# Token-halved first tiles, reordered loads, paired gate products and norm steps on another engine, in a fused state-space and gated-MLP kernel

## The chip, the cores and the metric

One core of one Trainium2 chip. The metric is the device time of one execution in microseconds (us), as the median of several executions. A profile of one execution goes with each kernel; its span (first to last instruction) is 1.8 to 1.9 us shorter than the time measured for that execution. Engines: PE is TensorE's matmuls, PEld its weight loads, DVE is VectorE, ACT is ScalarE, POOL is GpSimd, SP is SyncE, which issues the DMAs (SPq is its queue).

## The reference, cut to what matters

```python
# x: (1, 2048, 512); w_gate, w_up: (512, 1376); w_down: (1376, 512); all bfloat16
xn = layernorm(x)
# state-space layer: diagonal complex recurrence over 2048 tokens
Bu = xn @ (((Lam_bar - 1) / Lam)[:, None] * B).T
for t in range(L):
    h = Lam_bar * h + Bu[t]
s = 2 * (hseq @ C.T).real + xn * Dskip
g = silu((gelu(xn @ w_gate) * (xn @ w_up)) @ w_down)
return x + s * g
```

## The kernel before: the parts that matter

The 2048 tokens are four slabs of 512 (`TS`). In the loop over slabs, TensorE does, for slab s, 11 gate and up tiles of 128 features (`ffn`), and between them, after tiles 5, 7, 9 and 10, the four output matmul groups of slab s-1 (`y_mm`). Then come the scan input of slab s+1 (`u_ps`) and the down projection of slab s. ScalarE applies gelu and copies from PSUM, VectorE multiplies the two, scans, rotates and forms the outputs.

The head, slab 0: every tile of x is normalised, transposed on TensorE and copied to `xnT` before the first gate matmul:

```python
xs = [norm0(0), norm0(1)]
tps = [t_xn0(0, xs[0]), t_xn0(1, xs[1])]
xnT_out(nc.vector, 0, tps[0]); xnT_out(nc.scalar, 1, tps[1])
xs += [norm0(2), norm0(3)]
...                                   # tiles 2 and 3 the same way, then the first ffn
```

Slabs 2 and 3: ScalarE takes two sums per tile, and small steps (`ln_small`) make the scale and bias of the norm. For slab 1 VectorE takes the statistics. In all three ScalarE writes `xn`, and a DMA transposes it.

```python
def ln_out(s, m):
    ACT(out=xn[:], in_=x_tok[...], func=AF.Identity, scale=rs[...], bias=nb[...])
    nc.sync.dma_start_transpose(out=xnT[:, :, c0 : c0 + P], in_=xn[:])

def epi(s, m, y_ps, g2):
    def f():
        TT(out=yg[:], in0=y_ps[:, :], in1=g2[:], op=ALU.mult)
        TT(out=ot[:], in0=yg[:], in1=x_tok[:, s * M + m, :], op=ALU.add)
    dve(now() + 0.3, 0.95, f)
    nc.sync.dma_start(out=out_td[mg : mg + P, :], in_=ot[:])

# in the slab loop, after tile j
if 5 <= j < 5 + M:
    ln_out(s + 1, j - 5)
if j in (5, 7, 9, 10):
    epi(s - 1, m, y_mm(...), ...)
```

So the program order of SyncE's queue is, per slab: transpose 0, store 0, transposes 1 and 2, store 1, transpose 3, and so on.

VectorE's order is made when the kernel is built, by a small model of the two engines' clocks. Before an instruction asked for at `ready`, the helper places as much of the waiting scan and rotation work as the modelled clock allows:

```python
def drain(t, late):
    while waiting and max(clk["dve"], waiting[0][0]) + waiting[0][1] <= t + late:
        pop()                         # places a waiting scan or rotation step

def dve(ready, cost, f, late=0.8):
    drain(ready, late)
    clk["dve"] = max(clk["dve"], ready) + cost
    f()
```

Of the kernel before, what the change touches and what calls it, by code (L numbers as in the profile page):

```python
# [11 lines left out]
ALU = mybir.AluOpType  # L12
# [7 lines left out]
def kernel(  # L20
# [73 lines left out]
    def load_gu(i):  # L94
        a, b = CUTS[i], CUTS[i + 1]
        nc.sync.dma_start(out=wg[:, :, a:b], in_=wg_r[:, :, a:b])
        nc.sync.dma_start(out=wu[:, :, a:b], in_=wu_r[:, :, a:b])
# [8 lines left out]

    load_gu(0)
    load_gu(1)
    load_x(1)
    for h in range(2):  # L110
# [80 lines left out]
    ACT(out=pf[:], in_=pt_ps[:, :], func=AF.Copy)  # L191
    for a in (0, 2):
        for m in (a, a + 1):
            bn(0, m)
        for m in (a, a + 1):
            bn_end(0, m)
        rstd(0, a, a + 2)

    def xnT_out(eng, m, tp):
# [3 lines left out]
        else:  # L203
            eng.tensor_copy(out=o, in_=tp[:, :, :])

    xs = [norm0(0), norm0(1)]
    tps = [t_xn0(0, xs[0]), t_xn0(1, xs[1])]
    xnT_out(nc.vector, 0, tps[0])
    xnT_out(nc.scalar, 1, tps[1])
    xs += [norm0(2), norm0(3)]  # L210

    def second_half():
        tps.extend([t_xn0(2, xs[2]), t_xn0(3, xs[3])])
        xnT_out(nc.vector, 2, tps[2])
        xnT_out(nc.scalar, 3, tps[3])

    second_half()
    nc.gpsimd.tensor_tensor(out=dt_[:], in0=euler[:], in1=ldt, op=ALU.pow)
    STT(out=thn[:], in0=lim, scalar=1.0 / (2.0 * math.pi), in1=dt_[:], op0=ALU.mult, op1=ALU.mult)
# [5 lines left out]
    TSC(out=kr[:], in0=ang[:], scalar1=MAGIC, scalar2=MAGIC, op0=ALU.add, op1=ALU.subtract)  # L225
    TT(out=ang[:], in0=ang[:], in1=kr[:], op=ALU.subtract)
    STT(out=kr[:], in0=ang[:], scalar=-1.0, in1=ang[:], op0=ALU.mult, op1=ALU.max)
    ACT(out=sh[:], in_=ang[:], func=AF.Sin, scale=TWO_PI)
# [22 lines left out]
    diagI = consts.tile([P, KT, P], BF16, name="diagI")  # L251

    def coefficients():
        nre, nim, den, inv, t1, t2, t3, t4 = (
            small(n) for n in ("nre", "nim", "den", "inv", "t1", "t2", "t3", "t4")
        )
        TT(out=nre[:], in0=rho[:], in1=c1[:], op=ALU.mult)
        TT(out=nim[:], in0=rho[:], in1=s1[:], op=ALU.mult)
        TSC(out=nre[:], in0=nre[:], scalar1=-1.0, scalar2=None, op0=ALU.add)
        TT(out=den[:], in0=lre, in1=lre, op=ALU.mult)  # L260
        TT(out=t1[:], in0=lim, in1=lim, op=ALU.mult)
        TT(out=t2[:], in0=nim[:], in1=lim, op=ALU.mult)
        TT(out=t3[:], in0=nim[:], in1=lre, op=ALU.mult)
        TT(out=den[:], in0=den[:], in1=t1[:], op=ALU.add)
        TT(out=t1[:], in0=nre[:], in1=lre, op=ALU.mult)
        TT(out=t4[:], in0=nre[:], in1=lim, op=ALU.mult)
        nc.vector.reciprocal(out=inv[:], in_=den[:])
        TT(out=t1[:], in0=t1[:], in1=t2[:], op=ALU.add)
        TT(out=t3[:], in0=t3[:], in1=t4[:], op=ALU.subtract)
        TT(out=cre[:], in0=t1[:], in1=inv[:], op=ALU.mult)  # L270
        TT(out=cim[:], in0=t3[:], in1=inv[:], op=ALU.mult)
        TSC(out=cre[:], in0=cre[:], scalar1=2.0, scalar2=None, op0=ALU.mult)
        TSC(out=cim[:], in0=cim[:], scalar1=2.0, scalar2=None, op0=ALU.mult)
        TSC(out=ncre[:], in0=cre[:], scalar1=-1.0, scalar2=None, op0=ALU.mult)
        for kt in range(KT):
            TSC(out=diagI[:, kt, :], in0=ident_f[:], scalar1=dsk[:, kt : kt + 1], scalar2=None, op0=ALU.mult)

# [19 lines left out]
    def now():  # L297
        return clk["pe"]
# [120 lines left out]
    def ffn(s, j, at):  # L419
        cols = slice(s * TS, (s + 1) * TS)  # L420
        fs = min(P, F - j * P)
        fsl = slice(j * P, j * P + fs)
        g_ps = psum.tile([P, TS], FP32, name="g_ps", tag="ps")
        for kt in range(KT):
            nc.tensor.matmul(  # L425
                g_ps[:fs, :], lhsT=wg[:, kt, fsl], rhs=xnT[:, kt, cols], start=(kt == 0), stop=(kt == KT - 1)
            )
        u_ps = psum.tile([P, TS], FP32, name="up_ps", tag="ps")
        for kt in range(KT):
            nc.tensor.matmul(  # L430
                u_ps[:fs, :], lhsT=wu[:, kt, fsl], rhs=xnT[:, kt, cols], start=(kt == 0), stop=(kt == KT - 1)
            )
        pe_takes(2 * KT)
        gt = work.tile([P, TS], BF16, name="gt", tag="gt", bufs=4)
        ACT(out=gt[:fs], in_=g_ps[:fs, :], func=AF.Gelu_apprx_tanh)  # L435
        ub = work.tile([P, TS], BF16, name="ub", tag="ub", bufs=4)
        ACT(out=ub[:fs], in_=u_ps[:fs, :], func=AF.Copy)  # L437
        dve(now() + 0.9, 0.34, lambda: TT(out=at[:fs, j, :], in0=gt[:fs], in1=ub[:fs], op=ALU.mult))  # L438

# [69 lines left out]
    mq = consts.tile([P, NS, M], FP32, name="mq")  # L509
    nb = consts.tile([P, NS, M], FP32, name="nb")  # L510

    def ln_act(s, m):
# [4 lines left out]
    def ln_small(s):  # L517
        G = nc.gpsimd
        mean, var = sx[:, s, 0, :], sx[:, s, 1, :]
        G.tensor_scalar(out=mean, in0=mean, scalar1=1.0 / D, scalar2=None, op0=ALU.mult)  # L520
        G.tensor_tensor(out=mq[:, s, :], in0=mean, in1=mean, op=ALU.mult)
        G.tensor_scalar(out=var, in0=var, scalar1=1.0 / D, scalar2=EPS, op0=ALU.mult, op1=ALU.add)
        G.tensor_tensor(out=var, in0=var, in1=mq[:, s, :], op=ALU.subtract)
        G.tensor_tensor(out=rs[:, s, :], in0=var, in1=mhalf[:], op=ALU.pow)
        G.tensor_tensor(out=nb[:, s, :], in0=mean, in1=rs[:, s, :], op=ALU.mult)
        G.tensor_scalar(out=nb[:, s, :], in0=nb[:, s, :], scalar1=-1.0, scalar2=None, op0=ALU.mult)  # L526

# [6 lines left out]

    clk["pe"] = 9.0
    clk["dve"] = 10.5
    hsts, ats, g2s = {0: hst0}, {0: at0}, {}
# [6 lines left out]

    dve(11.5, 2.8, ln1_stats)
    G = nc.gpsimd
# [12 lines left out]
    for s in range(NS):  # L559
        for j in range(NFT):  # L560
            ffn(s, j, ats[s])
            if s == 0:
                if j == 0:
                    ca_wide()
                if j == 1:
                    dve(now(), 2.6, coefficients)
                if 3 <= j < 3 + M:
# [24 lines left out]
        if s < NS - 1:  # L592
            hsts[s + 1] = work.tile([P, 2, NPT, TS], BF16, name="hst", tag="hst")
            ats[s + 1] = work.tile([P, NFT, TS], BF16, name="at", tag="at")
            for h in range(2):
                chain(s + 1, h, u_pair(s + 1, h), hsts[s + 1])
            for m in range(M):
                g2s[s, m] = down(s, m, ats[s])
                if s == 0:
                    fold_c(m)  # L600
    s = NS - 1
    y0 = y_mm(s, 0, hsts[s])
# [37 lines left out]
```

## Time and profile before

| | before |
|---|---|
| time, median (lowest to highest) | 188.32 (188.29 to 188.4) us |
| span of the profiled run | 186.4 us |
| busy: TensorE / VectorE / ScalarE / GpSimd | 179.5 / 155.3 / 115.3 / 16.8 us |

TensorE is the bound: what it does not fill is lost. The prediction shows the lines for that. The columns of a timeline are start, length, engine and line, operation, operands; "..." marks lines left out, here and below.

### The profile page before, as it was taken

What the parts mean: (1) busy time and instruction counts of PE and PEld (TensorE: products, weight loads), DVE (VectorE), ACT (ScalarE), POOL (GpSimd) and SP (SyncE); (2) the same over time, 40 slices, a digit from 0 to 9 for tenths busy, and PEclk for the clock granted to TensorE, in tenths of its full rate; (3) what the DMA queues carried; (4) which work ended last, traced back from release to release, by engine and by line L of the source; (5) the groups of instructions that cost most, each with busy time, mean ns of one, the idle gap of its engine ahead of it and who ended that gap; (6) DMA issues with size and microseconds to landing.
All of it is one profiled execution on the core that took longest, in us unless ns stands there. A gap on an engine that the chain in (4) does not pass through costs nothing.

```text
span 186.4 us, 2533 instructions
## 1 busy us (share of the span) xinstructions
PE 179.5 (96%) x887; PEld 84.2 (45%) x887; DVE 155.3 (83%) x266; ACT 115.3 (62%) x208; POOL 16.8 (9%) x35
## 2 busy tenths in 40 slices
PE   7699999999999899999999999999999999999992
PEld 2344444444444344544444444544444444554452
DVE  4948999999977799999999999999999999532034
ACT  3289996677799979257259949747428733451210
POOL 3653000000000230000000080000000000000000
PEclk9999999999999999999999999999999999999999
DMA  5994924896000016200000003310000000000001
GB/s 147 336 306 105 223 49 92 221 250 203 0 0 0 0 24 91 58 28 28 0 0 5 2 0 77 91 30 29 0 0 0 0 4 28 28 30 28 32 28 57
DMA packets 24444, 12.26 MB, mean 66 GB/s; under 512 B 15760, under 2 KB 24432, under 8 KB 24432
## 3 DMA queue, kind: packets, MB, share of 16 engines
q1 hardware_dynamic: 24256, 12.03, 25.2%
q8 instruction: 7, 0.11, 0.3%
q10 hardware_dynamic: 176, 0.07, 0.1%
q14 instruction: 5, 0.04, 0.1%
HBM read 6.33 MB, written 2.10 MB: 45 GB/s over the span
## 4 chain that ended last, share of the span: by engine, by line
PE 88%; ACT 5%; DVE 4%; DMA 1%; issue 1%; ACTq 0%
PE f_ps L445 20%; PE g_ps L425 18%; PE up_ps L430 18%; PE u_ps L343 15%; PE y_ps L460 14%; PE y_ps L465 2%; ACT junk L515 1%; DVE st L154 1%; DMA x_tok<-in_A_x_dram 1%; PE y_ps L493 1%; ACT gt L435 1%; ACT ub L437 1%; ACT L435 1%; DVE qq L359 1%; PE tp L174 1%
## 5 line engine op out<-in xcount | busy, mean ns | idle before, releaser
L425 PE MATMUL g_ps<-xnT,wg 128*128 128x512 bf16 (+1 forms) x176 | 45.2, 379 | 0.7 <-ACT xnT L202 0.7
L430 PE MATMUL up_ps<-xnT,wu 128*128 128x512 bf16 (+1 forms) x176 | 45.2, 379 | 0.0
L445 PE MATMUL f_ps<-wd,at 128*128 128x512 bf16 (+1 forms) x176 | 38.7, 379 | 0.0
L435 ACT ACTIVATE gt<-g_ps 128x512 bf16<-128x512 f32 (+1 forms) x44 | 26.4, 600 | 11.1 <-PE g_ps L425 8.6
L389 DVE TENSOR_TENSOR_SCAN Ft<-rho,it,Wt 128x512 bf16<-128x512 f32 x24 | 30.1, 1274 | 0.0
L437 ACT ACTIVATE ub<-up_ps 128x512 bf16<-128x512 f32 (+1 forms) x44 | 26.5, 602 | 5.1 <-PE up_ps L430 4.9
L460 PE MATMUL y_ps<-C,hst 128*128 128x512 bf16 x120 | 28.7, 379 | 0.5 <-DVE hst L363 0.5
L343 PE MATMUL u_ps<-xnT,BT 128*128 128x512 bf16 x128 | 28.4, 379 | 0.0
L430 PEld LDWEIGHTS <-wu 128*128 128x128 bf16 (+1 forms) x176 | 17.6, 100 | 20.4
L445 PEld LDWEIGHTS <-at 128*128 128x128 bf16 (+1 forms) x176 | 17.2, 98 | 20.6
L348 ACT ACTIVATE U<-u_ps 128x512 bf16<-128x512 f32 x32 | 18.9, 610 | 11.1 <-PE u_ps L343 11.1
L425 PEld LDWEIGHTS <-wg 128*128 128x128 bf16 (+1 forms) x176 | 17.1, 100 | 19.0 <-issue 0.8
L438 DVE TENSOR_TENSOR at<-gt,ub 128x512 bf16<-128x512 bf16 (+1 forms) x44 | 18.0, 414 | 7.3 <-ACT ub L437 7.0
L450 ACT ACTIVATE g<-f_ps 128x512 f32<-128x512 f32 x16 | 9.6, 597 | 23.5 <-PE f_ps L445 23.5
L478 DVE TENSOR_TENSOR yg<-y_ps,g 128x512 bf16<-128x512 f32 x15 | 10.3, 684 | 13.7 <-PE y_ps L465 9.9
L343 PEld LDWEIGHTS <-BT 128*128 128x128 bf16 x128 | 12.4, 98 | 14.6
L460 PEld LDWEIGHTS <-hst 128*128 128x128 bf16 x120 | 11.5, 98 | 14.7 <-DVE hst L363 1.5
L530 ACT ACTIVATE xn<-x_tok,nb,rs 128x512 bf16<-128x512 bf16 x12 | 10.0, 832 | 3.8 <-POOL nb L526 3.8
L363 DVE TENSOR_TENSOR hst<-pp,qq 128x1024 bf16<-128x1024 bf16 x16 | 10.6, 688 | 0.2
L363 DVE TENSOR_TENSOR Wt<-pp,qq 128x1024 bf16<-128x1024 bf16 x16 | 10.5, 688 | 0.3
L515 ACT ACTIVATE junk<-x_tok 128x512 bf16<-128x512 bf16 x16 | 10.1, 630 | 0.3
L359 DVE TENSOR_TENSOR pp<-U,cos_b 128x2048 bf16<-128x2048 bf16 x8 | 9.8, 1223 | 0.3
(106 smaller groups left out, 145.0 us busy)
## 6 DMA issues: line engine op xcount, KB each, us to landing
out_dram<-ot SPq DMA_DIRECT2D x15, 128.0 KB, 1.7
x_tok<-in_A_x_dram SPq DMA_DIRECT2D x3, 512.0 KB, 6.9
wd<-in_B_w_down_dram SPq DMA_DIRECT2D x1, 1280.0 KB
wg<-in_B_w_gate_dram SPq DMA_DIRECT2D x1, 640.0 KB, 6.2
wu<-in_B_w_up_dram SPq DMA_DIRECT2D x1, 640.0 KB
wg<-in_B_w_gate_dram SPq DMA_DIRECT2D x1, 384.0 KB, 4.5
wu<-in_B_w_up_dram SPq DMA_DIRECT2D x1, 384.0 KB
wg<-in_B_w_gate_dram SPq DMA_DIRECT2D x1, 352.0 KB
```

Of the source, the lines that this page charges most:

```text
L343: nc.tensor.matmul(u_ps[:, :], lhsT=BT[:, ri, kt, pt * P : (pt + 1) * P], rhs=xnT[:, kt, cols], start=(kt == 0), stop=(kt == KT - 1),)
L348: ACT(out=U[:, ri, q, :], in_=u_ps[:, :], func=AF.Copy)
L363: return lambda: TT(out=dst()[i], in0=box["pp"][:, i, :, :], in1=box["qq"][:, 1 - i, :, :], op=op)
L389: nc.vector.tensor_tensor_scan(out=box["F"][:, ri, q, :], data0=rho[:, pt : pt + 1].to_broadcast([P, TS]), data1=box["W"][:, ri, q, :], in ...
L425: nc.tensor.matmul(g_ps[:fs, :], lhsT=wg[:, kt, fsl], rhs=xnT[:, kt, cols], start=(kt == 0), stop=(kt == KT - 1))
L430: nc.tensor.matmul(u_ps[:fs, :], lhsT=wu[:, kt, fsl], rhs=xnT[:, kt, cols], start=(kt == 0), stop=(kt == KT - 1))
L435: ACT(out=gt[:fs], in_=g_ps[:fs, :], func=AF.Gelu_apprx_tanh)
L437: ACT(out=ub[:fs], in_=u_ps[:fs, :], func=AF.Copy)
L438: dve(now() + 0.9, 0.34, lambda: TT(out=at[:fs, j, :], in0=gt[:fs], in1=ub[:fs], op=ALU.mult))
L445: nc.tensor.matmul(f_ps[:, :], lhsT=at[:fs, k, m0 : m0 + P], rhs=wd[:fs, k, :], start=(k == 0), stop=(k == NFT - 1))
L460: nc.tensor.matmul(y_ps[:, :], lhsT=hst[:, j // NPT, j % NPT, m0 : m0 + P], rhs=C2[:, j // NPT, j % NPT, :], start=(j == 0), stop=False,)
L515: ACT(out=junk[:], in_=x_tok[:, s * M + m, :], func=f, accum_out=sx[:, s, i, m : m + 1])
```

## The change

Its intent: start TensorE earlier, and take work from VectorE. The first two gate and up tiles are done in two halves of 256 tokens, so that the first halves run while tiles 2 and 3 of x are still being normalised. The x of slab 1 is loaded ahead of the second weight piece. Two gate tiles share one VectorE product of 1024 columns. The coefficients go to GpSimd (17 of 18 small steps; the reciprocal stays), the four skip diagonals to ScalarE. In exchange VectorE takes four short norm steps for each of slabs 2 and 3, which leaves GpSimd two where it had seven.

```diff
     load_gu(0)
+    load_x(1)
     load_gu(1)
-    load_x(1)
@@ head
+    for j in range(SPLIT):                       # SPLIT = 2
+        for up in range(2):
+            early[j, up] = gu_mm(0, j, up, 0, TS // 2)
+        if j == 0:
+            tps += [t_xn0(2, xs[2]), t_xn0(3, xs[3])]
+            xnT_out(nc.scalar, 3, tps[3])
   ...                                            # xnT_out(nc.vector, 2, ...) later
@@ coefficients: 17 small steps TT/TSC on VectorE -> GT/GS on GpSimd
@@ diagI: TSC on VectorE -> ACT(..., func=AF.Copy, scale=dsk[...])
@@ ffn
-        dve(now() + 0.9, 0.34, lambda: TT(out=at[:fs, j, :], in0=gt[:fs], in1=ub[:fs], op=ALU.mult))
+        if j == NFT - 1:
+            dve(now() + 0.9, 0.34, lambda: TT(...))              # the odd last tile
+        elif i:                                                  # every second tile
+            dve(now() + 0.9, 0.61, lambda: TT(out=at[:, j - 1 : j + 1, :], in0=gt[:], in1=ub[:], op=ALU.mult))
@@ ln_small
-        G.tensor_scalar(...)                      # seven steps on GpSimd
-        ...
+        def f():                                  # four steps on VectorE
+            STT(...); TSC(...); STT(...); TSC(...)
+        dve(now() + 1.0, 0.3, f)
+        nc.gpsimd.tensor_tensor(out=rs[:, s, :], in0=var, in1=mhalf[:], op=ALU.pow)
+        nc.gpsimd.tensor_tensor(out=nb[:, s, :], in0=nm[:, s, :], in1=rs[:, s, :], op=ALU.mult)
```

More of the change, by code (lines that the diff above doesn't have):

```diff
@@ L191 @@
     ACT(out=pf[:], in_=pt_ps[:, :], func=AF.Copy)
-    for a in (0, 2):
-        for m in (a, a + 1):
-            bn(0, m)
-        for m in (a, a + 1):
-            bn_end(0, m)
-        rstd(0, a, a + 2)
     def xnT_out(eng, m, tp):
@@ L204, in xnT_out @@
             eng.tensor_copy(out=o, in_=tp[:, :, :])
+    bn(0, 0)
+    bn(0, 1)
+    bn_end(0, 0)
+    bn_end(0, 1)
+    rstd(0, 0, 2)
+    nc.gpsimd.tensor_tensor(out=dt_[:], in0=euler[:], in1=ldt, op=ALU.pow)
+    bn(0, 2)
+    bn(0, 3)
     xs = [norm0(0), norm0(1)]
+    bn_end(0, 2)
+    bn_end(0, 3)
+    rstd(0, 2, 4)
     tps = [t_xn0(0, xs[0]), t_xn0(1, xs[1])]
@@ L210, with gu_mm @@
     xs += [norm0(2), norm0(3)]
-    def second_half():
-        tps.extend([t_xn0(2, xs[2]), t_xn0(3, xs[3])])
-        xnT_out(nc.vector, 2, tps[2])
-        xnT_out(nc.scalar, 3, tps[3])
-    second_half()
-    nc.gpsimd.tensor_tensor(out=dt_[:], in0=euler[:], in1=ldt, op=ALU.pow)
+    SPLIT = 2
+    early = {}
+    pair = {}
+    def gu_mm(s, j, up, a=0, b=TS, ps=None):
+        fs = min(P, F - j * P)
+        fsl = slice(j * P, j * P + fs)
+        if ps is None:
+            ps = psum.tile([P, TS], FP32, name="up_ps" if up else "g_ps", tag="ps")
+        w = wu if up else wg
+        for kt in range(KT):
+            nc.tensor.matmul(
+                ps[:fs, a:b], lhsT=w[:, kt, fsl], rhs=xnT[:, kt, s * TS + a : s * TS + b],
+                start=(kt == 0), stop=(kt == KT - 1),
+            )
+        return ps
+    for j in range(SPLIT):
[4 more added lines that the diff above has]
+            xnT_out(nc.scalar, 3, tps[3])
     STT(out=thn[:], in0=lim, scalar=1.0 / (2.0 * math.pi), in1=dt_[:], op0=ALU.mult, op1=ALU.mult)
@@ L226 @@
     TT(out=ang[:], in0=ang[:], in1=kr[:], op=ALU.subtract)
+    xnT_out(nc.vector, 2, tps[2])
     STT(out=kr[:], in0=ang[:], scalar=-1.0, in1=ang[:], op0=ALU.mult, op1=ALU.max)
@@ L251 @@
     diagI = consts.tile([P, KT, P], BF16, name="diagI")
-    def coefficients():
-        nre, nim, den, inv, t1, t2, t3, t4 = (
-            small(n) for n in ("nre", "nim", "den", "inv", "t1", "t2", "t3", "t4")
-        )
-        TT(out=nre[:], in0=rho[:], in1=c1[:], op=ALU.mult)
-        TT(out=nim[:], in0=rho[:], in1=s1[:], op=ALU.mult)
-        TSC(out=nre[:], in0=nre[:], scalar1=-1.0, scalar2=None, op0=ALU.add)
-        TT(out=den[:], in0=lre, in1=lre, op=ALU.mult)
-        TT(out=t1[:], in0=lim, in1=lim, op=ALU.mult)
-        TT(out=t2[:], in0=nim[:], in1=lim, op=ALU.mult)
-        TT(out=t3[:], in0=nim[:], in1=lre, op=ALU.mult)
-        TT(out=den[:], in0=den[:], in1=t1[:], op=ALU.add)
-        TT(out=t1[:], in0=nre[:], in1=lre, op=ALU.mult)
-        TT(out=t4[:], in0=nre[:], in1=lim, op=ALU.mult)
-        nc.vector.reciprocal(out=inv[:], in_=den[:])
-        TT(out=t1[:], in0=t1[:], in1=t2[:], op=ALU.add)
-        TT(out=t3[:], in0=t3[:], in1=t4[:], op=ALU.subtract)
-        TT(out=cre[:], in0=t1[:], in1=inv[:], op=ALU.mult)
-        TT(out=cim[:], in0=t3[:], in1=inv[:], op=ALU.mult)
-        TSC(out=cre[:], in0=cre[:], scalar1=2.0, scalar2=None, op0=ALU.mult)
-        TSC(out=cim[:], in0=cim[:], scalar1=2.0, scalar2=None, op0=ALU.mult)
-        TSC(out=ncre[:], in0=cre[:], scalar1=-1.0, scalar2=None, op0=ALU.mult)
-        for kt in range(KT):
-            TSC(out=diagI[:, kt, :], in0=ident_f[:], scalar1=dsk[:, kt : kt + 1], scalar2=None, op0=ALU.mult)
@@ new lines, with skip_diag @@
+    GT = nc.gpsimd.tensor_tensor
+    GS = nc.gpsimd.tensor_scalar
+    def skip_diag(kt):
+        ACT(out=diagI[:, kt, :], in_=ident_f[:], func=AF.Copy, scale=dsk[:, kt : kt + 1])
+    nre, nim, den, inv, t1, t2, t3, t4 = (
+        small(n) for n in ("nre", "nim", "den", "inv", "t1", "t2", "t3", "t4")
+    )
+    def coefficients():
+        GT(out=nre[:], in0=rho[:], in1=c1[:], op=ALU.mult)
+        GT(out=nim[:], in0=rho[:], in1=s1[:], op=ALU.mult)
+        GS(out=nre[:], in0=nre[:], scalar1=-1.0, scalar2=None, op0=ALU.add)
+        GT(out=den[:], in0=lre, in1=lre, op=ALU.mult)
+        GT(out=t1[:], in0=lim, in1=lim, op=ALU.mult)
+        GT(out=t2[:], in0=nim[:], in1=lim, op=ALU.mult)
+        GT(out=t3[:], in0=nim[:], in1=lre, op=ALU.mult)
+        GT(out=den[:], in0=den[:], in1=t1[:], op=ALU.add)
+        GT(out=t1[:], in0=nre[:], in1=lre, op=ALU.mult)
+        GT(out=t4[:], in0=nre[:], in1=lim, op=ALU.mult)
+        GT(out=t1[:], in0=t1[:], in1=t2[:], op=ALU.add)
+        GT(out=t3[:], in0=t3[:], in1=t4[:], op=ALU.subtract)
@@ L278, in fold_c, with coefficients_end @@
+    def coefficients_end():
+        nc.vector.reciprocal(out=inv[:], in_=den[:])
+        GT(out=cre[:], in0=t1[:], in1=inv[:], op=ALU.mult)
+        GT(out=cim[:], in0=t3[:], in1=inv[:], op=ALU.mult)
+        GS(out=cre[:], in0=cre[:], scalar1=2.0, scalar2=None, op0=ALU.mult)
+        GS(out=cim[:], in0=cim[:], scalar1=2.0, scalar2=None, op0=ALU.mult)
+        GS(out=ncre[:], in0=cre[:], scalar1=-1.0, scalar2=None, op0=ALU.mult)
     def fold_c(pt):
@@ L419, in ffn @@
     def ffn(s, j, at):
-        cols = slice(s * TS, (s + 1) * TS)
         fs = min(P, F - j * P)
-        fsl = slice(j * P, j * P + fs)
-        g_ps = psum.tile([P, TS], FP32, name="g_ps", tag="ps")
-        for kt in range(KT):
-            nc.tensor.matmul(
-                g_ps[:fs, :], lhsT=wg[:, kt, fsl], rhs=xnT[:, kt, cols], start=(kt == 0), stop=(kt == KT - 1)
-            )
-        u_ps = psum.tile([P, TS], FP32, name="up_ps", tag="ps")
-        for kt in range(KT):
-            nc.tensor.matmul(
-                u_ps[:fs, :], lhsT=wu[:, kt, fsl], rhs=xnT[:, kt, cols], start=(kt == 0), stop=(kt == KT - 1)
-            )
-        pe_takes(2 * KT)
-        gt = work.tile([P, TS], BF16, name="gt", tag="gt", bufs=4)
-        ACT(out=gt[:fs], in_=g_ps[:fs, :], func=AF.Gelu_apprx_tanh)
-        ub = work.tile([P, TS], BF16, name="ub", tag="ub", bufs=4)
-        ACT(out=ub[:fs], in_=u_ps[:fs, :], func=AF.Copy)
-        dve(now() + 0.9, 0.34, lambda: TT(out=at[:fs, j, :], in0=gt[:fs], in1=ub[:fs], op=ALU.mult))
+        if s == 0 and j < SPLIT:
+            g_ps, u_ps = (gu_mm(s, j, up, TS // 2, TS, early[j, up]) for up in range(2))
+        else:
+            g_ps, u_ps = gu_mm(s, j, 0), gu_mm(s, j, 1)
+        pe_takes(2 * KT)
+        i = j % 2
+        if i == 0:
+            pair["g"] = work.tile([P, 2, TS], BF16, name="gt", tag="gt", bufs=3)
+            pair["u"] = work.tile([P, 2, TS], BF16, name="ub", tag="ub", bufs=3)
+        gt, ub = pair["g"], pair["u"]
+        ACT(out=gt[:fs, i, :], in_=g_ps[:fs, :], func=AF.Gelu_apprx_tanh)
+        ACT(out=ub[:fs, i, :], in_=u_ps[:fs, :], func=AF.Copy)
+        if j == NFT - 1:
+            dve(now() + 0.9, 0.34, lambda: TT(out=at[:fs, j, :], in0=gt[:fs, 0, :], in1=ub[:fs, 0, :], op=ALU.mult))
+        elif i:
+            dve(now() + 0.9, 0.61, lambda: TT(out=at[:, j - 1 : j + 1, :], in0=gt[:], in1=ub[:], op=ALU.mult))
     def down(s, m, at):
@@ L510 @@
     nb = consts.tile([P, NS, M], FP32, name="nb")
+    nm = consts.tile([P, NS, M], FP32, name="nm")
     def ln_act(s, m):
@@ L517, in ln_small @@
     def ln_small(s):
-        G = nc.gpsimd
-        mean, var = sx[:, s, 0, :], sx[:, s, 1, :]
-        G.tensor_scalar(out=mean, in0=mean, scalar1=1.0 / D, scalar2=None, op0=ALU.mult)
-        G.tensor_tensor(out=mq[:, s, :], in0=mean, in1=mean, op=ALU.mult)
-        G.tensor_scalar(out=var, in0=var, scalar1=1.0 / D, scalar2=EPS, op0=ALU.mult, op1=ALU.add)
-        G.tensor_tensor(out=var, in0=var, in1=mq[:, s, :], op=ALU.subtract)
-        G.tensor_tensor(out=rs[:, s, :], in0=var, in1=mhalf[:], op=ALU.pow)
-        G.tensor_tensor(out=nb[:, s, :], in0=mean, in1=rs[:, s, :], op=ALU.mult)
-        G.tensor_scalar(out=nb[:, s, :], in0=nb[:, s, :], scalar1=-1.0, scalar2=None, op0=ALU.mult)
+        total, var = sx[:, s, 0, :], sx[:, s, 1, :]
+        def f():
+            STT(out=mq[:, s, :], in0=total, scalar=-1.0 / (D * D), in1=total, op0=ALU.mult, op1=ALU.mult)
+            TSC(out=nm[:, s, :], in0=total, scalar1=-1.0 / D, scalar2=None, op0=ALU.mult)
+            STT(out=var, in0=var, scalar=1.0 / D, in1=mq[:, s, :], op0=ALU.mult, op1=ALU.add)
+            TSC(out=var, in0=var, scalar1=EPS, scalar2=None, op0=ALU.add)
+        dve(now() + 1.0, 0.3, f)
+        nc.gpsimd.tensor_tensor(out=rs[:, s, :], in0=var, in1=mhalf[:], op=ALU.pow)
+        nc.gpsimd.tensor_tensor(out=nb[:, s, :], in0=nm[:, s, :], in1=rs[:, s, :], op=ALU.mult)
     def ln_out(s, m):
@@ L532, in ln_out @@
         nc.sync.dma_start_transpose(out=xnT[:, :, c0 : c0 + P], in_=xn[:])
-    clk["pe"] = 9.0
-    clk["dve"] = 10.5
+    clk["pe"] = 8.1
+    clk["dve"] = 10.3
     hsts, ats, g2s = {0: hst0}, {0: at0}, {}
@@ L543, in ln1_stats @@
             bn_end(1, m)
-    dve(11.5, 2.8, ln1_stats)
+    dve(10.3, 2.8, ln1_stats)
     G = nc.gpsimd
@@ L562 @@
             if s == 0:
-                if j == 0:
+                if j == 1:
                     ca_wide()
-                if j == 1:
-                    dve(now(), 2.6, coefficients)
+                    coefficients()
+                if j == 8:
+                    coefficients_end()
                 if 3 <= j < 3 + M:
@@ L600 @@
                     fold_c(m)
+                    skip_diag(m)
     s = NS - 1
```

## The prediction

> **What bounds the kernel now.** I read the busy slices first, then TensorE's own waits, then the chain of waits in order of time, then the timeline of the first 24 us and of 45 to 65 us. The slices of the page:
>
> ```profile
> PE   7699999999999899999999999999999999999992
> DVE  4948999999977799999999999999999999532034
> PEclk9999999999999999999999999999999999999999
> ```
>
> TensorE is full from the third slice to the last but one (a slice is 186.4 / 40 = 4.66 us), at the full clock: the end is set by when its matmul stream starts, by holes in it, and by a short tail. VectorE is full over long stretches too, which matters only if TensorE waits for it. TensorE's waits, as waiter, releaser, total, times and longest:
>
> ```profile
> PE w_ps L146 <- DVE halfpi L122: 1.2, 1, 1.2
> PE tp L174 <- DVE xn L165: 1.2, 2, 0.7
> PE g_ps L425 <- ACT xnT L202: 0.7, 1, 0.7
> PE y_ps L460 <- DVE hst L363: 0.5, 1, 0.5
> ```
>
> That is all. Three belong to the head: the first gate matmul waits until ScalarE has copied the last transposed tile of x (xnT). Only one is later: the first output matmul of slab 0 waits 0.5 us for hst. In the chain (start, length, piece):
>
> ```profile
> 7.79 0.73 PE tp L174 x8
> 9.19 1.02 PE g_ps L425 x4
> 10.21 0.86 PE up_ps L430 x4
> 11.08 0.86 PE g_ps L425 x4
> 11.94 0.86 PE up_ps L430 x4
> 12.80 0.86 PE g_ps L425 x4
> ...
> 61.05 1.15 DVE qq L359
> 62.22 0.70 DVE hst L363
> 62.97 1.04 PE y_ps L460 x4
> ```
>
> The stream starts at 9.19, and two gate and up tiles are through at 12.80; after that it is matmul upon matmul at 0.86 per four. From the timeline, the last matmul ends near 183.1, and product, add and store take the remaining 3.3 us. So at most two things can be won: the start (about 9.2) and the hole of 0.5. The measured 188.32 is 1.9 above the span; I keep that offset.
>
> **What the Trainium skill says.** "TensorE: Matmul & The Clock Gate", section "Back-to-back issue gap", gives N / 2.4 + 2.5 ns for a warm matmul: 215.8 ns for 512 columns and 109 for 256. The trace agrees: 0.86 / 4 = 0.216, and the 256-column output matmuls at the end (x8) take 0.87, 0.109 each. The same section's 131 ns for 512 columns in a real stream is not seen here. So halves cost no TensorE time.
>
> "VectorE: DVE Perf Modes", section "The TRN2 errata", says a fixed cost per instruction that one large tile pays once. The trace agrees:
>
> ```profile
> L438 DVE TENSOR_TENSOR at<-gt,ub 128x512 bf16<-128x512 bf16 x40 | 16.4, 414 | 6.0 <-ACT ub L437 5.8
> L363 DVE TENSOR_TENSOR hst<-pp,qq 128x1024 bf16<-128x1024 bf16 x16 | 10.6, 688 | 0.2
> ```
>
> 1024 columns cost 688 ns, two of 512 cost 828.
>
> "ScalarE: Activation LUTs", section "What ACT_TABLE_LOAD costs", has 1283 ns plus about 1380 of drain per switch. The trace has the 1283, but no such drain: the load starts at 11.29 and the first gelu at 12.59.
>
> "SBUF — State Buffer", section "Who interferes with whom", says that VectorE instructions with two SBUF inputs contend with GpSimd ones that read SBUF. It fits that the same power step on GpSimd takes 1037 ns in one place and 1466 on average in the slabs.
>
> **The change part by part.**
>
> *Head.* Before, VectorE does all statistics of slab 0 before the first norm (starts 6.08), and all four xnT tiles come before the first gate matmul. After, in steps from the timeline before (my estimate):
> - Statistics of tiles 2 and 3 end about 5.7, the first power is ready at 5.45: first norm 5.7 (was 6.08), second ends 6.43 (was 6.81).
> - From the end of a norm to its transposes done: 6.81 to 7.30, 0.49. So ScalarE copies tile 1 from 6.92 to 7.52, and the first half matmul starts at about 7.6.
> - Tile 0's gate and up halves: 8 x 0.109 + 0.16 for the cold start = 1.0, to 8.6.
> - The second power now stands behind the dt power on GpSimd (1.07) and behind the norms, so it ends near 7.7 (was 7.04); norms 2 and 3 end about 8.5, just before TensorE asks. Eight transposes to 9.1, tile 1's halves (0.87) to 10.0.
> - xnT 3 goes to ScalarE, 9.25 to 9.85. xnT 2 stands on VectorE behind the five angle steps (8.56 to 9.81 before, 1.25; now about 8.4 to 9.65), so it ends about 10.05.
> - Second halves start about 10.1 and take 16 x 0.109 = 1.74: two tiles are through at 11.85, against 12.80. **Gain 0.95**. The transposes are on the path once in both orders; what is won is that 1.9 us of matmuls fill the wait for tiles 2 and 3.
>
> *Loads.* Gate weights of the first cut land 4.5 after issue at 2.18, so at 6.7; the up weights behind them by about 7.8, from the 336 GB/s of that slice, and the up half needs them at 8.1. x of slab 1 (0.5 MB, landed at 12.75 before) moves ahead of the 1.28 MB of later weights: it lands at about 9.3, those at 11.2 and 12.9. They are first needed by tile 3 at about 13.6 and 14.4. Hidden, with 1.5 us to spare; VectorE can then start slab 1's statistics near 10.5 instead of 12.78.
>
> *VectorE.* Eighteen small coefficient steps and four diagonals leave it: 16.82 to 19.26, 2.4 us. Forty products become twenty: 16.4 - 20 x 0.688 = 2.6 us busy. Eight norm steps come, 8 x about 0.16 = 1.3. Net about -3.7, plus 2.3 from the earlier statistics. By adding the durations in the new order, I get slab 0's hst at about 57 (before: 64.0), while its first output matmul would ask at 61.9 - 0.95 = 61. In the new order hst also comes ahead of slab 1's first product, which now waits for ScalarE before it. **Gain 0.5, the hole.** All the rest of VectorE's relief is off the path and buys nothing.
>
> *ScalarE.* Four diagonals of 128x128: from 712 ns for 512 columns with a scale operand, less 384 x 0.833 = 320, some 390 ns each. Three fit in its idle 0.56 after each down block; the fourth delays slab 1's first gelu by about 0.3. Hidden, since TensorE has four tiles of PSUM lead there.
>
> *GpSimd.* Coefficients at 0.2 to 0.5 each, needed only at 45: hidden. Norm of the next slab: seven steps become two, after four short ones on VectorE; ScalarE waits for it (3.8 in total) off the path.
>
> Sum: 0.95 + 0.5 = 1.45; 188.32 - 1.45 = 186.87, **186.9**.
>
> **Rivals.**
> 1. *PSUM buffers become the wait.* The gelu table load ends at 12.59 in either order, since the sine steps end as before, so ScalarE empties tile 0 only at about 13.1, while tile 3 wants that bank at 13.6. Only 0.5 us spare. Likewise VectorE's order lets the output product of slab 1's last tile come near 83, with its bank asked for near 84. Either would return 0.2 to 0.8: 187.2 to 187.7. For it: thin margins. Against: before, TensorE waited for neither.
> 2. *Weights late.* If the up weights land at 9 rather than 7.8, or the displaced ones after 14, TensorE idles early and half of the head's gain goes: about 187.4. Against: no wait on a weight before, and bytes ahead of them are unchanged for the first cut.
> 3. *VectorE was the true limit, and its 4 us of relief count in full:* 184.5. Against: one hole of 0.5 in all of TensorE's stream after the head. I nearly exclude it.
> 4. *The pair product comes too late for the gate buffers* (three pairs instead of four singles): ScalarE would stall, then TensorE, time back to 188 or more. Against: the new order puts each pair's product at least a slab of pairs before its reuse.
>
> **Range and chances.** The two gains bound the result below: head at best 1.3 (no idle at 10.0 and an earlier first norm), with the hole 1.8, 186.5; a little is left for noise. Above, the head at 0.6 and one new wait of 0.3: 187.6. I take 186.3 to 187.7. Two per cent is 3.8 us, more than both gains together, and a loss of that size needs a stall that recurs in every slab. Hence 0.02 faster, 0.965 within, 0.015 slower.
>
> **What would show it.** In the changed profile: first gate half at 7.6 (not 9.2), third gate tile near 11.9 (not 12.8), with an idle below 0.3 us ahead of the second halves; slab 1's statistics without a wait for x; no wait of an output matmul for hst; last matmul near 181.6; VectorE's busy time some 3.5 lower with the end following only by 1.4. Wrong if TensorE's waits show ScalarE's gelu or a copy of tile 0 ahead of tile 3, a weight load, or a product holding a PSUM bank in slab 1 or 2; or if the hole at the first output matmul is still there.

## More of the kernel before

```profile
116.46 0.68 DVE L363 TENSOR_TENSOR Wt<-pp,qq 128x1024 bf16<-128x1024 bf16 x1
117.06 0.68 DVE L478 TENSOR_TENSOR yg<-y_ps,g 128x512 bf16<-128x512 f32 x1
117.10 0.84 ACT L530 ACTIVATE xn<-x_tok,nb,rs 128x512 bf16<-128x512 bf16 x1
...
118.12 1.28 DVE L389 TENSOR_TENSOR_SCAN Ft<-rho,it,Wt 128x512 bf16<-128x512 f32 x1
118.24 0.33 SPq L482 DMA_DIRECT2D out_dram<-ot  x1
...
118.66 1.19 SPq L532 DMA_TRANSPOSE xnT<-xn  x1
```

To be read: VectorE makes output tile 1 (`yg` at 117.06), the queue stores it at 118.24, and right behind it issues the last transpose of slab 3 at 118.66. The work on a slab's scan runs in two halves, each with four scans (half of the states each); the first scan of slab 2's second half comes after the product. TensorE starts the scan input of slab 3, which needs that transpose, at 122.41.

## The result and the profile after

The changed kernel takes 187.51 us (187.29 to 187.86, four executions) beside 188.33 (188.29 to 188.4) for the kernel before: 0.82 less, ratio 0.9958 with a 95% interval of 0.9941 to 0.9975. Every ratio here is the mean time of one kernel's runs over that of the other's of the same rounds, so not quite the ratio of the medians.

The time is in the predicted range, but the gain is little over half of the 1.45 foretold. Busy times, from the page's first part: TensorE 178.7, VectorE 151.6, ScalarE 116.0, GpSimd 23.8. TensorE's waits after (waiter, releaser, total, times, longest):

```profile
PE w_ps L146 <- DVE halfpi L122: 1.2, 1, 1.2
PE g_ps L226 <- ACT xnT L195: 0.7, 1, 0.7
PE u_ps L371 <- DMA xnT<-xn: 0.6, 1, 0.6
PE tp L174 <- DVE xn L165: 0.2, 1, 0.2
```

The wait for `hst` is gone. In its place stands one that was not there: the scan input waits for a DMA transpose of `xn`. The chain of waits shows where (start, length, piece):

```profile
118.08 0.67 PE up_ps L226 x4
118.74 2.48 DMA xnT<-xn
121.22 0.25 issue
121.47 7.07 PE u_ps L371 x32
```

From the timeline of each trace, the start of the same six pieces of TensorE's work tells when the gain came and went:

| start of | before | after | after ahead by |
|---|---|---|---|
| scan input of slab 0 | 19.55 | 18.56 | 0.99 |
| first output group of slab 0 | 61.87 | 60.88 | 0.99 |
| second output group of slab 0 | 68.17 | 66.29 | 1.88 |
| scan input of slab 2 | 79.20 | 77.52 | 1.68 |
| scan input of slab 3 | 122.41 | 121.47 | 0.94 |
| last half output group | 181.98 | 181.03 | 0.95 |

So: plus 0.99 in the head, plus 0.89 at the first output group, then minus 0.20 and minus 0.74 at two scan inputs. TensorE reached 1.88 and kept 0.95. (The profiled execution is the fastest of the four; the medians differ by 0.82.) The timeline of the changed kernel at the place of the larger loss, beside the one shown of before:

```profile
110.78 1.27 DVE L417 TENSOR_TENSOR_SCAN Ft<-rho,it,Wt 128x512 bf16<-128x512 f32 x1
...
113.01 2.45 DVE L417 TENSOR_TENSOR_SCAN Ft<-rho,it,Wt 128x512 bf16<-128x512 f32 x2
...
115.35 0.84 ACT L559 ACTIVATE xn<-x_tok,nb,rs 128x512 bf16<-128x512 bf16 x1
...
115.97 1.28 DVE L417 TENSOR_TENSOR_SCAN Ft<-rho,it,Wt 128x512 bf16<-128x512 f32 x1
...
117.16 0.67 DVE L504 TENSOR_TENSOR yg<-y_ps,g 128x512 bf16<-128x512 f32 x1
...
118.32 0.33 SPq L508 DMA_DIRECT2D out_dram<-ot  x1
...
118.74 1.19 SPq L561 DMA_TRANSPOSE xnT<-xn  x1
```

To be seen: `xn` of the last tile is written by 116.19 (115.35 + 0.84), 1.75 earlier than before (117.10 + 0.84). But its transpose is issued at 118.74, no earlier than before (118.66), because the store stands ahead of it in the queue and waits for VectorE's output tile. VectorE makes that at 117.16, although it has less to do: four scans that stood behind the product before now stand ahead of it. TensorE is done with its earlier work at 120.73 (the last output group starts at 118.78 and takes 1.95) and stands until 121.47. The smaller loss is of the same kind: there the last transpose of slab 2 was issued at 74.79, and 74.79 + 2.48 + 0.25 is 77.52, when that scan input started. Before, TensorE came at 122.41 and the transpose of slab 3, 2.48 after its issue, had landed with 1.3 us to spare.

### The profile page after: what moved, and what is told of

It is laid out like the page before. It is cut to its first block, busy times and chain, and to the rows that moved or that the text cites. A ratio compares the mean times of both kernels' runs of the same rounds, so it can differ in the third digit from the quotient of the medians. Undisturbed runs are those within 1.5% of the kernel's fastest.

```text
span 185.5 us, 2504 instructions
## 1 busy us (share of the span) xinstructions
PE 178.7 (96%) x887; PEld 85.8 (46%) x903; DVE 151.6 (82%) x233; ACT 116.0 (63%) x212; POOL 23.8 (13%) x42
## 4 chain that ended last, share of the span: by engine, by line
PE 84%; ACT 6%; DVE 4%; DMA 3%; issue 1%; POOL 0%
PE f_ps L471 20%; PE up_ps L226 18%; PE g_ps L226 17%; PE u_ps L371 13%; PE y_ps L486 13%; ACT gt L459 2%; PE y_ps L491 2%; ACT ub L460 2%; DMA xnT<-xn 1%; DVE st L154 1%; DMA x_tok<-in_A_x_dram 1%; ACT xn L559 1%; PE y_ps L519 1%; DVE xn L165 1%; ACT L459 1%
## 5 line engine op out<-in xcount | busy, mean ns | idle before, releaser
L226 PE MATMUL g_ps<-xnT,wg 128*128 128x512 bf16 (+2 forms) x179 | 44.8, 369 | 0.8 <-ACT xnT L195 0.7
L226 PE MATMUL up_ps<-xnT,wu 128*128 128x512 bf16 (+2 forms) x181 | 45.2, 370 | 0.3
L417 DVE TENSOR_TENSOR_SCAN Ft<-rho,it,Wt 128x512 bf16<-128x512 f32 x24 | 29.3, 1266 | 0.0
L486 PE MATMUL y_ps<-C,hst 128*128 128x512 bf16 x117 | 28.2, 379 | 0.2
L226 PEld LDWEIGHTS <-wu 128*128 128x128 bf16 (+1 forms) x184 | 18.3, 100 | 19.7
L226 PEld LDWEIGHTS <-wg 128*128 128x128 bf16 (+1 forms) x184 | 17.8, 100 | 18.4 <-issue 0.8
L464 DVE TENSOR_TENSOR at<-gt,ub 128x1024 bf16<-128x1024 bf16 x20 | 13.7, 684 | 9.8 <-ACT ub L460 9.8
L554 POOL TENSOR_TENSOR rs<-sx,mhalf 128x4 f32<-128x4 f32 x2 | 3.2, 1594 | 72.6 <-DVE sx L551 42.2
```

The source lines that it names most:

```text
L226: nc.tensor.matmul(ps[:fs, a:b], lhsT=w[:, kt, fsl], rhs=xnT[:, kt, s * TS + a : s * TS + b], start=(kt == 0), stop=(kt == KT - 1),)
L417: nc.vector.tensor_tensor_scan(out=box["F"][:, ri, q, :], data0=rho[:, pt : pt + 1].to_broadcast([P, TS]), data1=box["W"][:, ri, q, :], in ...
L464: dve(now() + 0.9, 0.61, lambda: TT(out=at[:, j - 1 : j + 1, :], in0=gt[:], in1=ub[:], op=ALU.mult))
L486: nc.tensor.matmul(y_ps[:, :], lhsT=hst[:, j // NPT, j % NPT, m0 : m0 + P], rhs=C2[:, j // NPT, j % NPT, :], start=(j == 0), stop=False,)
```

## The experiments

My theory: the head and the closed hole are worth 1.9 together, and 0.9 of it is given back by the order store, then transpose, in SyncE's queue. Rivals: the two gains were smaller than thought, or the pairs, the load order or the norm steps cost time themselves. "Before" in the table is the kernel before, run in the same rounds.

| kernel | median (lowest to highest), us | before | ratio [95%] |
|---|---|---|---|
| the change | 187.51 (187.29 to 187.86) | 188.33 | 0.9958 [0.9941, 0.9975] |
| 1 store behind the transpose | 186.58 (186.39 to 186.9) | 188.44 | 0.9901 [0.9888, 0.9914] |
| 2 head alone | 187.64 (187.22 to 188.04) | 188.44 | 0.9955 [0.9943, 0.9967] |
| 3 head undone | 188.40 (188.28 to 189.03) | 188.44 | 1.0000 [0.9987, 1.0014] |
| 4 store moved in the kernel before | 188.56 (188.24 to 188.75) | 188.44 | 1.0004 [0.9992, 1.0016] |
| 5 norm steps back on GpSimd | 189.79 (189.71 to 190.24) | 188.74 | 1.0066 [1.0051, 1.0081] |
| 6 output products sooner | 186.68 (186.53 to 186.75) | 188.74 | 0.9895 [0.9882, 0.9908] |
| 7 as 1, fewer warm-up matmuls | 186.59 (186.49 to 188.43) | 188.74 | 0.9909 [0.9881, 0.9938] |
| 8 single gate products | 186.64 (186.41 to 187.14) | 188.74 | 0.9897 [0.9881, 0.9914] |
| 9 both 1 and 8 | 186.60 (186.44 to 186.9) | 188.48 | 0.9902 [0.9887, 0.9916] |
| 10 load order undone | 187.60 (187.42 to 189.04) | 188.48 | 0.9977 [0.9934, 1.0019] |
| 11 both 1 and 5 | 188.67 (188.6 to 188.97) | 188.48 | 1.0012 [0.9998, 1.0027] |
| 12 as 1, head undone | 187.67 (187.38 to 188.08) | 188.48 | 0.9956 [0.9942, 0.997] |

**1. The store behind the last transpose.**

```diff
-                    epi(s - 1, m, ...)           # sends the store at once
+                    held = epi(s - 1, m, ..., hold=(m == 1))
+                if j == 8:                       # after the last transpose was issued
+                    held()
```

> The changed kernel, with one store moved: in slabs 1 and 2 the store of output tile 1 is issued after the last transpose of the next slab's normed x, not ahead of it. Nothing else moves. Theory (queue): the last transpose waits in the in-order DMA queue behind a store that waits for VectorE's product, so the scan input matmuls of the next slab wait; then the 0.6 wait of u_ps for xnT goes, and 0.75 at slab 2 plus 0.15 to 0.2 at slab 1 come back: about 186.6. Rival (norm): xn itself or the transpose is late; then the wait stays and the time is 187.5. Rival (VectorE): something else slow; no change.

Measured: 186.58, as the theory had it, and TensorE's wait for the transpose is not in its profile. The queue now reads:

```profile
113.86 3.88 SPq L567 DMA_TRANSPOSE xnT<-xn  x3
...
117.47 0.67 DVE L504 TENSOR_TENSOR yg<-y_ps,g 128x512 bf16<-128x512 f32 x1
...
118.63 0.33 SPq L510 DMA_DIRECT2D out_dram<-ot  x1
...
120.83 1.46 PE L371 MATMUL u_ps<-xnT,BT 128*128 128x512 bf16 x6
```

The product is even later (117.47), but the three transposes no longer wait for it: the last is issued before 117.74. This shows the cause of the lost 0.9.

**4. The same move in the kernel before.** The same edit.

> The kernel before with the same one store moved behind the last transpose. Queue theory: there the transpose lands some 1.5 us ahead of need, so nothing is won: 188.3 within 0.1. If the move of the store helps by itself (for example by easing the queue in general), it is faster by 0.3 or more.

Measured: 188.56, ratio 1.0004. The order in the queue cost nothing as long as TensorE came late; it is the change that made it a wait.

**2 and 3. The head alone, and all but the head.**

```diff
# 2: the kernel before with
+    SPLIT = 2 ... early[j, up] = gu_mm(0, j, up, 0, TS // 2) ...
# 3: the changed kernel with the head of the kernel before
-    SPLIT = 2
+    SPLIT = 0
# cut in both: the order of slab 0's statistics and norms, the start values of the modelled clocks
```

> The kernel before, with the head alone changed (order of slab 0's statistics and norms, dt power earlier, first two tiles in token halves). Queue theory: the first 1.13 us are won, the hole of 0.5 to 0.7 at the first output matmul stays, and the last transpose lands just in time (121.1 against 121.45), so 187.2: the part alone beats the whole. Rival (gain of the whole is just a smaller head and hole): well above 187.3, or the part is not faster than the whole.

> The changed kernel with the head undone, all else kept (load order, pairs, norm steps, coefficients on GpSimd). Queue theory: only the hole of about 0.67 closes, the transposes have about 0.8 to spare, so 187.65. Rival (relief of VectorE counts in full): 186 or less. Rival (the rest costs time): 188.3 or more.

Measured: 187.64 for the head alone, 0.80 under the kernel before; its only later wait is still the first output group for `hst` (0.5 in the list). I expected 187.2, which was too much. It ties with the whole change rather than beating it. Without the head: 188.40, no gain at all, where I expected 187.65. That was a miss, and the trace of run 3 says why. The hole at the first output group is closed (62.48 to 67.88 is 5.40, before 61.87 to 68.17 was 6.30: 0.90 won). But the scan inputs of slabs 2 and 3 stand 0.19 and 0.73, together 0.92, since the product of VectorE comes later than in the kernel before (118.74, before 117.06):

```profile
118.74 0.66 DVE L501 TENSOR_TENSOR yg<-y_ps,g 128x512 bf16<-128x512 f32 x1
...
119.89 0.33 SPq L505 DMA_DIRECT2D out_dram<-ot  x1
...
120.32 1.19 SPq L558 DMA_TRANSPOSE xnT<-xn  x1
...
123.04 2.32 PE L368 MATMUL u_ps<-xnT,BT 128*128 128x512 bf16 x10 [0.57 <-DMA xnT<-xn]
```

So the wait does not come from the head. The rest of the change brings it: there 0.90 is won and 0.92 lost.

**12. All but the head, with the store moved.** The edits of 3 and 1. It measures the hole by itself.

> The changed kernel with the head undone and the store of output tile 1 behind the last transpose: what is left of the change is the relief of VectorE alone, without the wait it brought in. Theory: the step from the first output matmul of slab 1 to the second was 6.30 us before the change and 5.40 in every kernel where that hole is closed, so the hole was worth 0.90, and the two waits at the scan inputs of slabs 2 and 3 (0.19 and 0.73 in the trace of the run with only the head undone) are gone: 0.9 under the kernel before, 187.6 us, give or take 0.2. Rival (the hole is worth only the 0.5 that the list of waits shows, as the prediction had it): 187.95 to 188.1 us.

Measured: 187.67, 0.81 under the kernel before, at the theory's figure and not at the rival's. Against run 3, which differs in the store alone, 0.73 is won back. In its trace the step between the first two output groups is 5.40, and no scan input waits. Which part of the relief closes the hole is not shown: it stays closed with the norm steps (run 5), the pairs (8) or the load order (10) undone one at a time, and the coefficients and diagonals were never undone alone.

**6. Output products earlier on VectorE.** The order in the queue stays; the product is placed before more of the waiting work.

```diff
-        dve(now() + 0.3, 0.95, f)
+        dve(now() + 0.3, 0.95, f, late=-1.7)
```

> The changed kernel, with the output products placed one to two pieces of work earlier in VectorE's order (the store stays ahead of the last transpose). Queue theory: product and store of tile 1 come at least 1 us sooner, the wait for xnT goes, 186.6 to 186.9. Rival (the store's place in the DMA queue as such, not VectorE, is what delays): 187.5.

Measured: 186.68, as expected. It attacks the same wait from the other end, and two scans stand ahead of the product instead of four:

```profile
112.24 2.45 DVE L417 TENSOR_TENSOR_SCAN Ft<-rho,it,Wt 128x512 bf16<-128x512 f32 x2
...
115.20 0.68 DVE L504 TENSOR_TENSOR yg<-y_ps,g 128x512 bf16<-128x512 f32 x1
...
116.79 1.19 SPq L561 DMA_TRANSPOSE xnT<-xn  x1
```

**8. Pairs undone.**

```diff
-            dve(now() + 0.9, 0.61, lambda: TT(out=at[:, j - 1 : j + 1, :], in0=gt[:], in1=ub[:], op=ALU.mult))
+        dve(now() + 0.9, 0.34, lambda: TT(out=at[:fs, j, :], in0=gt[:fs], in1=ub[:fs], op=ALU.mult))
# cut: the buffers, three of 1024 columns in the changed kernel, four of 512 here
```

> The changed kernel with the pairs undone: one gate tile per VectorE product again, four buffers. VectorE gets some 2.6 us of busy time back. Theory (VectorE's relief is off the path except through the order of its queue): hole at the first output matmul still closed, wait for xnT between 0.3 and 1.2, so 187.3 to 187.9. Rival (pairs are what closed the hole): the 0.5 wait of y_ps for hst is back, 188.

Measured: 186.64. A miss, and an instructive one: taking the pairs away makes the changed kernel 0.9 faster. VectorE is busy 153.2 us instead of 151.6, and still the product stands at 115.96 with two scans ahead of it, the last transpose is issued at 117.54, and TensorE waits for none. A replay of the helper from the kernel's code, without the chip, gives the same counts: four scans ahead of the product in the changed kernel, two here. It points to what the model is told, not to the number of requests: with single products charged at 0.305 each, half of a pair's 0.61, four scans stand ahead again.

**9. Both.** The edits of 1 and 8.

> The changed kernel with both undoings that were faster alone: the gate products single again, and the store of output tile 1 of each slab issued after the last transpose. Theory (both take away the same wait, the first matmul of the scan input of slab 3 standing behind the last transpose of xn; each alone brought 186.6): together no more than one of them, 186.4 to 186.7 us. Rival (the pairs cost something of their own besides the queue): the two add up, under 186.1 us.

Measured: 186.60, no more than either alone. Three different edits (1, 6, 8) and this sum all end at 186.6 to 186.7. So they take away one and the same wait, and no cost of the pairs apart from it is seen.

**10. The load order undone.**

```diff
-    load_x(1)
     load_gu(1)
+    load_x(1)
```

> The changed kernel with x of slab 1 loaded behind the second weight piece again. VectorE then stands some 2.6 us at the statistics of slab 1, as it did before the change (2.57 us in that trace). Theory: it catches up in the slack it has until 62 us (it idles 1.47 and 0.98 us at two gate products there), and the wait at the end of slab 2 stays as it is: 187.5 us, give or take 0.3. Rival (the load order is what closes the hole at the first output matmul, since it is the largest single relief of VectorE in slab 0): the wait of the first output matmul for hst is back, about 0.5, and the time is 188.0 or more.

Measured: 187.60, with one execution at 189.04 which I cannot explain. VectorE stands 2.52 us for x of slab 1, the hole stays closed and the scan input waits 0.61, as in the changed kernel. So no worth of the load order is seen, though with that execution the interval is wide.

**5 and 11. The norm steps back on GpSimd, without and with the store moved.** The seven steps of the kernel before in place of the six of the changed one.

> The changed kernel with one part undone: the seven norm steps of the next slab are on GpSimd again. Theory (the norm steps cost VectorE its lead): in the changed kernel VectorE stands in order behind these steps in slab 1, which wait for ScalarE's sums (0.98 and 0.51 of idle near 62 to 63.6), and from there it works without a gap to the product of output tile 1 in slab 2 (53.5 us later); without them that product and its store come 1.0 to 1.5 earlier, the last transpose lands before 120.7, the wait of u_ps for xnT goes: 186.7. Rival (moving the norm steps gained, as was meant): xn comes later by some 1.5 and the wait stays or grows: 187.5 to 188.

> The run with the seven norm steps back on GpSimd (189.79 us), with the store of output tile 1 moved behind the last transpose as well. Theory from that run's trace: the loss goes through ScalarE, which stands 4.46 us in its own order until GpSimd has finished the seven steps, so the gelus and copies behind it are late, a gate matmul waits 1.22 us for a PSUM buffer, and a gate product holds up the scan input of slab 2 by 0.7 us; the transposes only cost 0.3 us. So moving the store wins back 0.3 at most: 189.4 to 189.7 us. Rival (the loss goes through the transposes, as in the changed kernel): near 187.5 us or below.

Measured: 189.79 and 188.67. I expected 186.7 of the first: my largest miss. The norm steps, which I took for hidden, cost 2.1 us or more when they are on GpSimd in the changed kernel (11 against 1: 188.67 to 186.58). From the timeline of run 5:

```profile
64.45 1.02 POOL L548 TENSOR_TENSOR mq<-sx 128x4 f32<-128x4 f32 x1
...
65.56 1.09 POOL L549 TENSOR_SCALAR sx<-sx 128x4 f32<-128x4 f32 x1
...
70.72 0.81 ACT L557 ACTIVATE xn<-x_tok,nb,rs 128x512 bf16<-128x512 bf16 x1 [4.46 <-POOL nb L553]
...
71.44 0.58 ACT L459 ACTIVATE gt<-g_ps 128x512 bf16<-128x512 f32 x1
...
72.07 1.02 PE L226 MATMUL g_ps<-xnT,wg 128*128 128x512 bf16 x4 [1.22 <-ACT gt L459]
```

Beside VectorE's scans and products a 128x4 step on GpSimd took 0.57 to 1.12 us, and the seven took 7.0 (63.65 to 70.69); before the change they took 3.7 at the same place (63.62 to 67.28), though the power step took 1.04 in both. That the scans are what slows them fits the trace but was not tested by itself. ScalarE stood 4.46 us at `xn`. The gelu behind it in program order came late, at 71.44, though the matmuls of its gate tile had ended by 66.32, and TensorE waited 1.22 for that PSUM buffer.

The second loss of run 5 teaches how to read a releaser. Its list of TensorE's waits says that the scan input of slab 2 waited 0.7 for VectorE's product `at`. But the last transpose was issued at 77.58; with the 2.48 to landing and 0.25 of issue, as in the chain shown above, that makes 80.31, to the hundredth when the scan input started. Moving the store in run 11 took that wait away and won 1.1 of the 2.3, where I had allowed 0.3. The other half, the wait of 1.22 for the PSUM buffer, is still in its list. The transpose was the true releaser, and my expectation had taken the label at its word.

**7. Fewer warm-up matmuls, with the store moved.**

```diff
-    dummies(5)
+    dummies(2)
```

> The changed kernel with the store moved (186.58 before) and two instead of five warm-up matmuls after the parameter transpose. In two profiles of other kernels of this study the 14 warm-up matmuls ended at 7.4 instead of 5.9, all of them at half speed, and the first transposes, ready at 6.1 to 6.6, waited for them. Theory (warm-up in the way): the slow starts lose less; median lower by 0.1 to 0.4 and a narrower spread, 186.2 to 186.5. Rival (the clock is released later with less activity, and real matmuls run at half speed): 187 or more.

Measured: 186.59, against 186.58 for run 1 on another chip, and one of six executions at 188.43, with a granted clock of 0.988 where the others have 0.999 or more. No gain, and perhaps a risk; this stays open. The slow warm-ups that the expectation gives fit runs 2 and 3, where the 14 matmuls ended at 7.42 and 7.33 (5.89 in the kernel before); but not quite all ran at half speed, for the shortest took 494 and 407 ns, where most took 634 and the fastest of the kernel before 379.

## Why the prediction was right and where it failed

The forecast of no change by 2% and the range were right, the range partly by luck. The hole was worth 0.39 more than thought, and that made good a part of the 0.94 that the new waits cost. With the hole at 0.5, as foretold, the same terms give 188.32 - 0.99 - 0.5 + 0.94 = 187.8, outside the range. None of the signs of being wrong that it lists came in the changed kernel's profile; it listed none for the DMA queue. By its steps:

- **Head, gain 0.95: right.** 0.99 on the trace, and not by the chance of one profile: the scan input of slab 0 starts at 19.55 to 20.16 in the four profiles with the old head and at 18.56 to 19.39 in the nine with the new one and all warm-up matmuls, 0.96 apart in the mean. The first half matmul started at 7.58 (foretold 7.6), the second halves at 9.90 (10.1), with an idle of under 0.3 ahead of them. Run 2 gives 0.80 in the medians. Its profile, of the slowest of its six executions, had a slower warm-up, with first transposes at 7.25 instead of 6.18; whether that holds for the median is not shown.
- **Loads, hidden: right.** The statistics of slab 1 started at 10.03 without a wait. Run 10 shows that the order was not needed. But the margin for the up weights is thin: in the profiles of runs 1 and 6 TensorE waited 0.2 for them, the second rival in small. The first rival is near too: the changed kernel's chain of waits runs through ScalarE from 10.15 to 22.85, where a matmul takes over at 22.88, so a still earlier start would probably have met ScalarE's copies there.
- **"Gain 0.5, the hole": the mechanism right, the term too small.** `hst` was ready at 56.1 (foretold about 57), and the output group started at 60.88 (61). The term measured 0.89, not 0.5, and run 12 gives 0.81 in the medians. I took the figure from the list of waits. In the timeline of before, the group's first two matmuls start at 61.87, so the third was due at 62.30 and came at 62.97 (0.67). The seventh, due at 63.83, came with the last piece of `hst` at 64.05 (0.22). The list does not count what the modelled end of the matmuls before covers, and it named only one of two waits.
- **"All the rest of VectorE's relief is off the path and buys nothing": the step that failed.** Beyond the hole it bought nothing, and it cost 0.94: waits of 0.20 and 0.74 at the scan inputs of slabs 2 and 3. The freed time was filled at build time with scans placed ahead of output tile 1, so that the product stayed at 117.1 while TensorE came up to 1.9 earlier. (In the replay of the helper, taking the 2.6 charged for the coefficients off the kernel before is enough to put four scans ahead of the product, where it has none.) The store that waits for that product stands ahead of the last transpose. I followed the product only to its PSUM bank (rival 1) and the transpose only to ScalarE. No rival named the queue that joins them. Runs 1, 6 and 8 each remove the wait and end at 186.6; runs 3 and 12 differ in it alone.
- **GpSimd, "off the path": true** of the two steps left, and of the seven in the kernel before, where no wait of TensorE names them. It is not true of the seven in the changed kernel (runs 5 and 11). Moving them with the rest was a benefit that I did not see.
- **GpSimd's coefficients at 0.2 to 0.5 each: too small.** Several took 1.0 to 1.24. They ended at 33.8, needed at 45: hidden, as said.
- **ScalarE's diagonals at 390 ns: right**, 389 measured, beside 713 for 512 columns: (713 - 389) / 384 = 0.84 ns per column. VectorE's busy time fell by 3.7, as worked out, though with 17 coefficient steps leaving and not eighteen.
- **The upper end, 187.6**, is a slip: 0.6 + 0.5 - 0.3 = 0.8 gives 187.5.

The sum as it should have read: 0.99 + 0.89 - 0.94 = 0.94 on the trace, and 0.82 in the medians. The best version, the change with the store behind the last transpose, takes 186.58: 1.0% under the kernel before and 0.5% under the changed one.

## What to carry to other kernels

When the bounding engine moves forward, every transfer that was in time "with slack" must be checked again, and with it the program order of the queue that issues it: here a store that waited for a late result held back the transpose behind it (ready at 116.19, issued at 118.74). Not tested: sending the stores of the slab loop from another engine's queue. Time freed on an engine whose order is made by a model is not simply idle; look at what the model puts there, and ahead of what. Size a hole by the distance between two like pieces of work in the timeline of both kernels, and check a releaser against the landing times of the DMAs before believing its name.

## What the Trainium skill lacked or had wrong

- "DMA: Bandwidth & Descriptors", section "Issuing engines are not separate DMA queues", says that issuing from several engines saves only the time to initiate a DMA. No run here tests that. The section does not warn (I say it of this section, not of the whole skill) that a DMA whose data is late holds back those behind it on the same issuing engine. Here a transpose whose input was ready at 116.19 was issued at 118.74; with the store moved, the kernel went from 187.51 to 186.58 us.
- "SBUF — State Buffer", section "Who interferes with whom", has the contention of two-input VectorE instructions with GpSimd, and the runs fit it, without a test of its own. It gives no figure for a chain of tiny steps: the shortest 128x4 steps took 0.20 us, others (powers aside) up to 1.24, and the chain of seven went from 3.7 to 7.0 us.
- "TensorE: Matmul & The Clock Gate", section "Back-to-back issue gap": its 131 ns per 512-column matmul in a real stream was not seen; the unbroken stretches read here ran at 216 ns (32 in 6.91 us), the page's figure for an isolated one.
- The same page, section "What's actually happening", says that the warm-up varies from run to run because its window runs free. The runs fit: nine warm-up matmuls took 3.42 to 4.02 us. The page puts the whole penalty under 1% of a typical span, and 1.07 us of 186 between the earliest and the latest first transposes (6.18 and 7.25) is within that. What it doesn't say is that this can be more than the gain under study, here 0.82.
- "ScalarE: Activation LUTs", section "What ACT_TABLE_LOAD costs": the drain of about 1380 ns was not seen. The load started at 11.20 and the first gelu at 12.49, after 1.29 us.
